# Four attention layers on one core: the output projection read from dense rows, half the side credit in the last layer, and a rule for unread matmuls

## The chip, the cores and the metric

The kernel runs on one core of a Trainium2 chip. The metric is the device time of one execution in microseconds (us). Three runs of the kernel before took 2326.96, 2328.76 and 2332.97 us; the median is 2328.76 us.

## The reference

The input is x, 2048 tokens of 640 features in bf16. Four layers are added to it in turn, and each is layer norm, attention with 32 heads of 20 features, an output projection, and the residual sum:

```python
def _B_ref(x, wqkv, wo):
    qkv = (x @ wqkv).reshape(B, S, 3, H, Dh) ...          # H = 32, Dh = 20
    scores = jnp.einsum("bhqd,bhkd->bhqk", q, k) * (Dh ** -0.5)
    p = _softmax(scores, axis=-1)
    o = jnp.einsum("bhqk,bhkd->bhqd", p, v)
    return o.transpose(0, 2, 1, 3).reshape(B, S, D) @ wo

x = x + _A_ref(_layernorm(x, axis=-1), A_wqkv, A_wo)      # a mask: 0 <= q - k < 256
x = x + _B_ref(_layernorm(x, axis=-1), B_wqkv, B_wo)      # all keys
x = x + _A_ref(_layernorm(x, axis=-1), A_wqkv, A_wo)
x = x + _B_ref(_layernorm(x, axis=-1), B_wqkv, B_wo)
```

The first and third layers (numbered 0 and 2 below, weights A) see a sliding window of 256 keys; the second and fourth (1 and 3, weights B) see all 2048 keys.

## The kernel before

**Tiling.** The tokens are cut into four chunks of 512 queries (c = 0 to 3), the heads into eight groups of four (g = 0 to 7). A unit is one (layer, chunk, group). Inside a group each head has a strip of 32 partitions: rows 0 to 19 of the strip hold its features, the other twelve are zeros. For one head and 128 keys, a score matmul (line 1253) writes a bank of PSUM of 128 keys x 512 queries. A "tile" is three such banks (two in part of layers 0 and 1, sometimes four in layer 3). One activation on ScalarE (line 1284) takes the exponential of a whole tile, and a second matmul with the values (line 1317) adds it up in bank 7. The value matrix carries a column of ones, so the sum of the exponentials comes with it. Banks 0 to 2 and 3 to 5 take turns as the tile's banks: TensorE fills one set while ScalarE reads the other. Bank 6 alone is left for everything else from the middle of layer 1 on.

**The end of a unit.** `finish_unit` copies bank 7 to `oT` (line 839), and a "tail" (`t_tail`, line 1006) divides by the sums in three steps with small matmuls, ending in a multiplication on VectorE that writes group g of the tile `on` (line 1052).

**The output projection.** `t_out` (line 529) multiplies the eight groups of `on` with the output weights `wop`. Both keep the strips of 32 with their zeros, so the contraction over 640 features is done as eight matmuls of 128 rows of which 80 are in use. A chunk is four blocks of 128 tokens by two halves of 320 columns, 64 matmuls of 128x320 in eight groups of eight (line 541). Every group takes bank 6, and VectorE adds it to x (line 550). For the very last chunk `t_before_last` (line 564) does groups 0 to 5 ahead of the end, and `t_out` the two that remain.

**What sets the order.** Everything is emitted by one loop over tiles. In each turn it emits the tile's score matmuls and its exponential; then `pump` lets the side tasks (projections, layer norm, output projection) run for as long as a credit lasts, which grows by `rate(t)` in each tile; then `keep_clock` runs; then come the value matmuls of earlier tiles. A side task that is inside an accumulation is "held" and is continued whatever the credit, so that the eight matmuls of a group of `t_out` stand in one tile. A task may ask to sleep for some ticks; a tick is one tile.

**Unread matmuls.** `keep_clock` (line 632) counts the TensorE work of the side tasks in a number `heat`. Where `heat` and what was carried over stay under `least` (1.76 for a tile of three banks from layer 1's second half on, 0 from the second chunk of layer 3 on), it adds matmuls of 128x512 whose result nobody reads (`unread`, line 620), as long as bank 6 is free.

**Loads.** The SP queue issues, in the program's order, the loads of queries, keys and values of coming units (lines 745 to 767), the output weights (line 132) and the result (line 556). The POOL queue issues the weights of the projections and the stores of q, k and v.

Of the kernel before, what the change touches and what calls it, by code (L numbers as in the profile page):

```python
# [12 lines left out]
ALU = mybir.AluOpType  # L13
ACT = mybir.ActivationFunctionType

P = 128
# [3 lines left out]
DH = 20  # L20
NT = S // P
KD = D // P
G = 8
C = 512
NC = S // C
EPS = 1e-5
SCALE = DH ** -0.5
HD = D // 2
# [21 lines left out]
def kernel(  # L50
# [75 lines left out]
        nc.sync.dma_start(out=x_sb[:, 4 * c : 4 * c + 4, :], in_=xin[:, 4 * c : 4 * c + 4, :])  # L126
    nc.sync.dma_start(out=wv_sb[1][:], in_=wq_view[1][:, :, 2 * D : 3 * D])

    def load_wop(w):
        v = wo_in[w].rearrange("(g j e) f -> j e g f", g=G, j=4)  # L130
        for j in range(4):
            nc.sync.dma_start(out=wop[32 * j : 32 * j + DH, :, :], in_=v[j])
# [41 lines left out]
    ready = set()  # L174
    todo = []
    tails = []
    state = {"tick": 0, "held": None, "credit": 0.0, "early": True, "act": True, "unit": 0, "heat": 0.0, "carry": 0.0, "least": 0.0}

    class Task:

# [348 lines left out]
    def t_out(l, c):  # L529
        on = ons[l, c]  # L530
        last = (l, c) == (3, NC - 1)
        while last and "before_last" not in ready:
            yield ("wait", 1)
        assert out_seq[out_n[0]] == l % 2
        for qb in range(4):
            for i in range(2):
                mb = yield from take_m()
                yp = ps[:, mb, 0:HD]
                g0 = G - 2 if last else 0
                for g in range(g0, G):  # L540
                    nc.tensor.matmul(  # L541
                        yp, lhsT=on[:, g, qb * P : (qb + 1) * P],
                        rhs=wop[:, g, i * HD : (i + 1) * HD],
                        start=(g == g0), stop=(g == G - 1),
                    )
                    if g < G - 1:
# [3 lines left out]
                nc.vector.tensor_tensor(out=xv, in0=had, in1=yp, op=ALU.add)  # L550
                drop_m(mb)
                yield ("pe", 0.14)
            if l < 3:
                stats(l + 1, c, qb)
            else:
                nc.sync.dma_start(out=xout[:, 4 * c + qb, :], in_=x_sb[:, 4 * c + qb, :])
        ons.pop((l, c))
        ready.add(("out", l, c))
        ready.add(("x", l + 1, c))
        n = out_n[0] = out_n[0] + 1  # L560
        if n < len(out_seq) and out_seq[n] != out_seq[n - 1]:
            load_wop(out_seq[n])

    def t_before_last():

        on = ons[3, NC - 1]
        for qb in range(4):
            for i in range(2):
                mb = yield from take_m()
                yp = ps[:, mb, 0:HD]  # L570
                for g in range(G - 2):
                    nc.tensor.matmul(
                        yp, lhsT=on[:, g, qb * P : (qb + 1) * P],
                        rhs=wop[:, g, i * HD : (i + 1) * HD],
                        start=(g == 0), stop=(g == G - 3),
                    )
                    if g < G - 3:
# [35 lines left out]

    def cool():

        return state["heat"] + state["carry"] < state["least"]

    def unread(b):

        nc.tensor.matmul(  # L620
            ps[:, b, :], lhsT=ident[:], rhs=masks[:, 0, :], start=True, stop=True
        )
        state["heat"] += 1.0
# [8 lines left out]
    def keep_clock():  # L632

        while cool():
            t = choose(False)
            if t is not None and state["credit"] > -0.5:
                state["credit"] -= advance(t)
                continue
            b = min(mfree, key=mfree.get)
            if mfree[b][0] > state["tick"]:  # L640
                break
            unread(b)
        spare = state["heat"] + state["carry"] - state["least"]
        state["carry"] = min(max(spare, 0.0), 3.0)
        state["heat"] = 0.0
# [360 lines left out]
    def t_tail(l, c, g, on, oT):  # L1006
# [40 lines left out]
        for qb in range(4):  # L1047
# [16 lines left out]
    def t_zeros():  # L1064

        z = ka_all[:, G : G + 4, :].rearrange("p a b -> p (a b)")
        yield ("wait", 4)
        for n in range(2):
            nc.gpsimd.dma_start(
                out=wop[:, 4 * n : 4 * n + 3, :].rearrange("p g f -> p (g f)"), in_=z[:, 0 : 3 * D]  # L1070
            )
            nc.gpsimd.dma_start(out=wop[:, 4 * n + 3, :], in_=z[:, 0:D])
            yield ("wait", 1)
        load_wop(0)
# [71 lines left out]
    with tc.manual_schedule():  # L1146
# [49 lines left out]
        def rate(t):  # L1196

            if t >= len(tiles):
                return 0.9
            u = tiles[t][0][0]  # L1200
            if index[u.l, u.c, u.g, u.part] < woven:
                return 1.2
            done, r = 0.0, 0.6 if state["early"] else 0.3
            for task in todo:
                done += max(task.left, 0.0)
                if task.need < len(units):
                    r = max(r, done / max(starts[id(units[task.need])] - t - 16, 1))
            return min(1.1 * r, 1.0 if u.l == 0 else 0.9)
# [10 lines left out]
        while ended is None or t < ended + 8:  # L1219
# [3 lines left out]
            if t < len(tiles) or banks:  # L1223
# [23 lines left out]
                if n_b == 4:  # L1247
                    mseq[0] += 1
                    mfree[6] = (state["tick"] + 2, mseq[0])
                for n in range(2):  # L1250
                    for i, (u, j, m, b0, subs, first, last, end) in enumerate(cur):
                        for kc, q0, qn, col in subs[n : n + 1]:
                            nc.tensor.matmul(  # L1253
                                sp[:, i, col * P : (col + qn) * P],
                                lhsT=u.k(kc, j), rhs=u.q(j, q0, qn), start=True, stop=True,
                            )
# [137 lines left out]
```

## Time and profile before

| | |
|---|---|
| profiled execution | 2335.83 us |
| its span, first to last instruction | 2334.1 us |
| ScalarE (ACT) busy | 2177.3 us, 93% |
| TensorE (PE) busy | 2019.9 us, 87% |
| VectorE (DVE) busy | 1465.6 us, 63% |
| mean granted TensorE clock | 0.852 |
| output projection, line 541 | 976 matmuls of 128x320 |
| unread matmuls, line 620 | 788 of 128x512 |

A busy time is the union of an engine's recorded instructions. The profile records an instruction with its whole latency, so that neighbours overlap; how fast an engine goes is read from the distance between starts. "PEclk" is the share of full speed that TensorE's clock was granted. A line of the waits names who waited, for whom, the sum in us, how often, and the longest.

### The profile page before, as it was taken

The numbers are of one execution on the slowest core, as the hardware profiler recorded it, in microseconds if no ns is written. First come the engines' busy times: TensorE is split into PE (matmuls) and PEld (weight loads), VectorE is DVE, ScalarE is ACT, GpSimd is POOL, SyncE is SP. The second block draws the span as 40 slices with busy tenths as digits, with TensorE's granted clock in tenths as the row PEclk, the third lists the DMA queues.
The fourth block names the chain that finished last, engine by engine and source line by source line (L and its number), as shares of the span: only waits on it lengthen the run. The fifth ranks groups of instructions, "written<-read, shape, count | busy, mean of one in ns | idle before, by whom it ended". The sixth has DMA issues, their size and how long they took to land.

```text
span 2334.1 us, 40627 instructions
## 1 busy us (share of the span) xinstructions
PE 2019.9 (87%) x15793; PEld 725.3 (31%) x15793; DVE 1465.6 (63%) x2726; ACT 2177.3 (93%) x1751; POOL 273.7 (12%) x445
## 2 busy tenths in 40 slices
PE   8899999988899888888988898898878888888887
PEld 3344333333323332233322333342322122222222
DVE  6677776426646666666666544452677777777772
ACT  6788889999999998999899899999999999999997
POOL 4332321201100012000120013001000000000000
PEclk9999999999989999999999999999855565556556
DMA  6232322322200123102230023112200010011100
GB/s 189 82 88 79 100 75 64 83 64 65 83 19 27 46 69 95 48 14 55 75 103 25 18 84 107 39 27 78 64 29 27 27 38 27 27 38 37 29 14 12
DMA packets 84881, 132.57 MB, mean 57 GB/s; under 512 B 19760, under 2 KB 60080, under 8 KB 84688
## 3 DMA queue, kind: packets, MB, share of 16 engines
q1 hardware_dynamic: 65472, 76.80, 11.9%
q0 software_dynamic: 19216, 53.17, 7.9%
q8 instruction: 124, 2.03, 0.4%
q14 instruction: 69, 0.57, 0.1%
HBM read 98.70 MB, written 27.79 MB: 54 GB/s over the span
## 4 chain that ended last, share of the span: by engine, by line
ACT 41%; PE 28%; issue 14%; DVE 12%; DMA 1%; POOL 0%; SPq 0%; ACTq 0%; DVEq 0%; POOLq 0%
ACT pt L1284 40%; PE ps L1253 7%; PE ps L354 5%; PE ps L541 4%; PE ps L1317 4%; DVE pt L1353 3%; PE ps L455 3%; PE ps L620 2%; DVE st L304 1%; DVE on L1052 1%; ACT ka L1284 1%; DVE raw_o L887 1%; DVE oT L839 1%; PE ps L419 1%; DVE raw_o L897 1%
## 5 line engine op out<-in xcount | busy, mean ns | idle before, releaser
L1284 ACT ACTIVATE pt<-ps 128x1536 bf16<-128x1536 f32 (+2 forms) x1641 | 2100.2, 1502 | 114.8 <-PE ps L1253 107.0
L1253 PE MATMUL ps<-qt,kt 32*128 32x512 bf16 x4008 | 642.1, 456 | 192.8 <-ACT pt L1284 160.9
L1317 PE MATMUL ps<-pt,vt 128*21 128x512 bf16 x3860 | 466.9, 456 | 0.3 <-ACT pt L1284 0.3
L1253 PEld LDWEIGHTS <-kt 32*128 32x128 bf16 x4008 | 190.4, 94 | 610.8 <-issue 589.7
L1353 DVE TENSOR_TENSOR pt<-pt,masks 128x1024 bf16<-128x1024 bf16 (+5 forms) x403 | 238.0, 624 | 127.3 <-ACT pt L1284 126.8
L620 PE MATMUL ps<-masks,ident 128*128 128x512 bf16 x788 | 270.6, 396 | 28.3 <-DVE rT L1039 11.9
L354 PE MATMUL ps<-xnT,wqk 128*128 128x512 bf16 x830 | 220.2, 390 | 14.2 <-DVE on L1052 3.7
L1317 PEld LDWEIGHTS <-vt 128*21 128x21 bf16 x3960 | 100.0, 90 | 319.8 <-issue 310.6
L304 DVE CAST st<-ps 128x512 bf16<-128x512 f32 x128 | 88.4, 690 | 159.9 <-PE ps L354 159.7
L541 PE MATMUL ps<-wop,on 128*128 128x320 bf16 x976 | 167.6, 315 | 5.5 <-DVE x_sb L550 2.3
L1253 PE MATMUL ps<-qa,ka 32*128 32x384 bf16 (+2 forms) x1408 | 117.6, 277 | 30.6 <-ACT pt L1284 25.8
L887 DVE TENSOR_SCALAR xnT<-ps 128x512 int32<-128x512 f32 x88 | 60.8, 690 | 106.6 <-PE ps L880 106.2
L1052 DVE TENSOR_TENSOR on<-oT,ps 128x512 bf16<-128x512 bf16 x128 | 87.3, 682 | 59.9 <-PE ps L1048 57.3
L839 DVE CAST oT<-ps 128x512 bf16<-128x512 f32 x112 | 76.7, 685 | 73.4 <-PE ps L1317 49.1
L550 DVE TENSOR_TENSOR x_sb<-x_sb,ps 128x320 bf16<-128x320 bf16 x120 | 57.9, 482 | 100.3 <-PE ps L541 100.0
L455 PE MATMUL ps<-wv,xnT 128*128 128x320 bf16 x640 | 108.6, 302 | 10.4 <-DVE rz L1025 3.8
L541 PEld LDWEIGHTS <-on 128*128 128x128 bf16 x976 | 90.5, 101 | 71.6 <-issue 37.3
L354 PEld LDWEIGHTS <-wqk 128*128 128x128 bf16 x830 | 71.0, 98 | 110.4 <-issue 52.2
L620 PEld LDWEIGHTS <-ident 128*128 128x128 bf16 x788 | 59.3, 97 | 130.5 <-issue 128.6
L388 POOL TENSOR_SCALAR rstd<-mv 128x4 f32<-128x4 f32 x15 | 4.9, 328 | 794.1 <-DVE mv L375 794.1
L1317 PE MATMUL ps<-pt,va 128*21 128x384 bf16 (+2 forms) x1408 | 79.5, 283 | 6.9 <-DVE pt L1353 5.5
L1253 PEld LDWEIGHTS <-ka 32*128 32x128 bf16 x1408 | 44.3, 92 | 98.2 <-issue 89.8
(107 smaller groups left out, 1794.4 us busy)
## 6 DMA issues: line engine op xcount, KB each, us to landing
vt<-v_d SPq DMA_DIRECT2D x48, 336.0 KB
kt<-k_d SPq DMA_DIRECT2D x192, 80.0 KB
wqk<-in_B_wqkv_dram POOLq DMA_DIRECT2D x80, 160.0 KB, 3.9
wqk<-in_A_wqkv_dram POOLq DMA_DIRECT2D x70, 160.0 KB, 3.5
k_d<-st POOLq DMA_DIRECT2D x75, 128.0 KB, 2.2
q_d<-st POOLq DMA_DIRECT2D x75, 128.0 KB, 2.2
qt<-q_d SPq DMA_DIRECT2D x384, 20.0 KB
v_d<-vs POOLq DMA_DIRECT2D x16, 336.0 KB, 3.1
```

What stands on the lines that cost most here:

```text
L304: nc.vector.tensor_copy(out=out_, in_=in_)
L354: nc.tensor.matmul(pq, lhsT=wt[:, dc, :], rhs=xt[:, dc, :], start=(dc == 0), stop=(dc == KD - 1),)
L455: nc.tensor.matmul(pv, lhsT=xt[:, dc, i * P : (i + 1) * P], rhs=wv_sb[l % 2][:, dc, h * HD : (h + 1) * HD], start=(dc == 0), stop=(dc == K ...
L541: nc.tensor.matmul(yp, lhsT=on[:, g, qb * P : (qb + 1) * P], rhs=wop[:, g, i * HD : (i + 1) * HD], start=(g == g0), stop=(g == G - 1),)
L620: nc.tensor.matmul(ps[:, b, :], lhsT=ident[:], rhs=masks[:, 0, :], start=True, stop=True)
L839: nc.vector.tensor_copy(out=oT[:], in_=op)
L887: V.tensor_scalar(out=xi.bitcast(I32)[:, i * C : (i + 1) * C], in0=side["psum"], scalar1=SCALE * LOG2E * E23, scalar2=127.0 * E23, op0=ALU ...
L1052: nc.vector.tensor_tensor(out=on[:, g, :], in0=oT[:], in1=zb, op=ALU.mult)
L1253: nc.tensor.matmul(sp[:, i, col * P : (col + qn) * P], lhsT=u.k(kc, j), rhs=u.q(j, q0, qn), start=True, stop=True,)
L1284: nc.scalar.activation(out=pt[:, i:k, b0 * P :], in_=sp[:, i:k, b0 * P :], func=ACT.Exp, scale=SCALE,)
L1317: nc.tensor.matmul(op[32 * j : 32 * j + VW, q0 * P : (q0 + qn) * P], lhsT=u.v(kc, j), rhs=pg[:, i, col * P : (col + qn) * P], start=(first ...
L1353: nc.vector.tensor_tensor(out=pt_[:, i:k, b0 * P :], in0=pt_[:, i:k, b0 * P :], in1=mv_, op=ALU.mult,)
```

## The change

Four things are changed.

1. From layer 1 on, `on` holds the 640 features densely, as five blocks of 128 rows. The multiplication at the end of a tail writes one of three free slots of `on` (5 to 7), and two ticks later SP issues four or five transfers within SBUF that move each head's 20 rows to their dense place (a head that crosses a block's edge takes two). After the last group of a chunk three more ticks pass before the chunk counts as done. `t_out` then needs five matmuls in a group where it had eight, and `t_before_last` four where it had six. The last two groups of the last chunk keep the old form. `load_wop` loads the weights densely from then on.
2. In the last layer the side tasks' credit grows by 0.45 in a tile where it grew by 0.9.
3. `cool` has a second rule: from the second chunk of layer 1 on, until `least` is 0, a tile whose own work is under 0.9 gets an unread matmul, whatever was carried over from earlier tiles.
4. Where bank 6 is not free for an unread matmul, it is "owed", and is emitted in front of the next tile's score matmuls, into the first of the banks that they are about to write.

```diff
-    def load_wop(w):
+    def packed(l, c):
+
+        return l > 0
+
+    def load_wop(w, dense):
+        if dense:
+            nc.sync.dma_start(out=wop[:, 0:KD, :], in_=wo_in[w].rearrange("(b p) f -> p b f", p=P))
+            if w and out_n[0] == 4:
+                v = wo_in[w].rearrange("(g j e) f -> j e g f", g=G, j=4)
+                for j in range(4):
+                    nc.sync.dma_start(
+                        out=wop[32 * j : 32 * j + DH, G - 2 : G, :], in_=v[j][:, G - 2 : G, :]
+                    )
+            return
...
+        dense = packed(l, c) and not last
+        a, b = (0, KD) if dense else (G - 2 if last else 0, G)
         for qb in range(4):
             for i in range(2):
...
-                for g in range(g0, G):
+                for g in range(a, b):
...
-        if n < len(out_seq) and out_seq[n] != out_seq[n - 1]:
-            load_wop(out_seq[n])
+        if n < len(out_seq) and (n == 4 or out_seq[n] != out_seq[n - 1]):
+            load_wop(out_seq[n], n >= 4)
...
-                for g in range(G - 2):
+                for b in range(4):
+                    n = min(P, (G - 2) * 80 - b * P)
...
     def cool():
 
+        if state["least"] > 0.0 and state["heat"] < state["floor"]:
+            return True
         return state["heat"] + state["carry"] < state["least"]
...
             b = min(mfree, key=mfree.get)
-            if mfree[b][0] > state["tick"]:
+            if state["early"] and mfree[b][0] > state["tick"]:
                 break
-            unread(b)
+            if mfree[b][0] > state["tick"] - (0 if state["early"] else 0):
+                state["owed"] += 1
+                state["heat"] += 1.0
+            else:
+                unread(b)
...
-        nc.vector.tensor_tensor(out=on[:, g, :], in0=oT[:], in1=zb, op=ALU.mult)
+        end = (l, c) == (3, NC - 1) and g >= G - 2
+        spread = packed(l, c) and not end
+        nu = on[:, 5 + g % 3 if spread else g, :]
+        nc.vector.tensor_tensor(out=nu, in0=oT[:], in1=zb, op=ALU.mult)
         drop_m(mb)
         yield ("pe", 0.3)
         fill(3)
+        if spread:
+            yield ("wait", 2)
+            for j in range(4):
+                r, a = (4 * g + j) * DH, 0
+                while a < DH:
+                    b, o = divmod(r + a, P)
+                    n = min(DH - a, P - o)
+                    nc.sync.dma_start(
+                        out=on[o : o + n, b, :], in_=nu[32 * j + a : 32 * j + a + n, :]
+                    )
+                    a += n
+            if g == G - 1 or (l, c, g) == (3, NC - 1, G - 3):
+                yield ("wait", 3)
...
             if t >= len(tiles):
-                return 0.9
+                return 0.45
...
+                while state["owed"]:
+                    state["owed"] -= 1
+                    nc.tensor.matmul(
+                        sp[:, 0, :], lhsT=ident[:], rhs=masks[:, 0, :], start=True, stop=True
+                    )
...
+                state["floor"] = 0.9 if state["unit"] >= index[1, 1, 0, None] else 0.0
```

More of the change, by code (lines that the diff above doesn't have):

```diff
@@ L176 @@
     tails = []
-    state = {"tick": 0, "held": None, "credit": 0.0, "early": True, "act": True, "unit": 0, "heat": 0.0, "carry": 0.0, "least": 0.0}
+    state = {"tick": 0, "held": None, "credit": 0.0, "early": True, "act": True, "unit": 0, "heat": 0.0, "carry": 0.0, "least": 0.0, "floor": 0.0, "owed": 0}
     class Task:
@@ L538, in t_out @@
                 yp = ps[:, mb, 0:HD]
-                g0 = G - 2 if last else 0
-                for g in range(g0, G):
+                for g in range(a, b):
                     nc.tensor.matmul(
@@ L543, in t_out @@
                         rhs=wop[:, g, i * HD : (i + 1) * HD],
-                        start=(g == g0), stop=(g == G - 1),
+                        start=(g == a), stop=(g == b - 1),
                     )
-                    if g < G - 1:
+                    if g < b - 1:
                         yield ("hold", 0.14)
@@ L570, in t_before_last @@
                 yp = ps[:, mb, 0:HD]
-                for g in range(G - 2):
+                for b in range(4):
+                    n = min(P, (G - 2) * 80 - b * P)
                     nc.tensor.matmul(
-                        yp, lhsT=on[:, g, qb * P : (qb + 1) * P],
-                        rhs=wop[:, g, i * HD : (i + 1) * HD],
-                        start=(g == 0), stop=(g == G - 3),
+                        yp, lhsT=on[0:n, b, qb * P : (qb + 1) * P],
+                        rhs=wop[0:n, b, i * HD : (i + 1) * HD],
+                        start=(b == 0), stop=(b == 3),
                     )
-                    if g < G - 3:
+                    if b < 3:
                         yield ("hold", 0.14)
@@ L1073, in t_zeros @@
             yield ("wait", 1)
-        load_wop(0)
+        load_wop(0, False)
         for t in (*kts, *qts):
```

## The prediction

> **What bounds the kernel now.** I read the page first: the busy shares, the chain that ended last and the groups.
>
> ```profile
> PE 2019.9 (87%) x15793; PEld 725.3 (31%) x15793; DVE 1465.6 (63%) x2726; ACT 2177.3 (93%) x1751; POOL 273.7 (12%) x445
> PEclk9999999999989999999999999999855565556556
> ACT 41%; PE 28%; issue 14%; DVE 12%; DMA 1%; POOL 0%; SPq 0%; ACTq 0%; DVEq 0%; POOLq 0%
> L1284 ACT ACTIVATE pt<-ps 128x1536 bf16<-128x1536 f32 (+2 forms) x1641 | 2100.2, 1502 | 114.8 <-PE ps L1253 107.0
> L541 PE MATMUL ps<-wop,on 128*128 128x320 bf16 x976 | 167.6, 315 | 5.5 <-DVE x_sb L550 2.3
> ```
>
> ScalarE's exponentials are the bound, and the only thing that holds them up is TensorE being late with scores: 107.0 us over the span. No change to TensorE's work can give more than what ScalarE loses there. The clock row says that TensorE runs at half clock in most of the last 30%, yet ScalarE is full in those slices. So I asked where the loss lies, by stretches (columns: PE, PEld, DVE, ACT, POOL busy, clock, DMA share, GB/s).
>
> ```profile
> 583.50:700.20 116.70, 102.99 (x771) 33.54 (x768) 62.60 (x117) 109.27 (x94) 11.30 (x16) 0.93 0.18 51
> 700.20:816.90 116.70, 102.01 (x855) 38.85 (x855) 76.13 (x151) 115.95 (x101) 3.31 (x6) 1.00 0.14 37
> 1700.00:1888.00 188.00, 154.74 (x956) 38.25 (x956) 142.04 (x205) 188.00 (x138) 0.00 (x0) 0.50 0.10 29
> 1888.00:1912.00 24.00, 21.56 (x157) 9.39 (x156) 17.51 (x26) 18.92 (x15) 0.00 (x0) 0.84 0.13 43
> ```
>
> In the last layer ScalarE is 188.00 of 188 busy at half clock with no side work, and 18.92 of 24 where a chunk's output projection runs. In layers 1 and 2 two stretches of equal length lose 7.4 us at clock 0.93 and 0.75 us at 1.00. The timeline of ScalarE prices the first kind:
>
> ```profile
> 1885.58 5.71 ACT L1284 ACTIVATE pt<-ps 128x1536 bf16<-128x1536 f32 x4
> 1892.91 1.45 ACT L1284 ACTIVATE pt<-ps 128x1536 bf16<-128x1536 f32 x1 [1.62 <-PE ps L1253]
> 1894.76 1.45 ACT L1284 ACTIVATE pt<-ps 128x1536 bf16<-128x1536 f32 x1 [0.39 <-PE ps L1253]
> 1896.60 8.34 ACT L1284 ACTIVATE pt<-ps 128x1536 bf16<-128x1536 f32 x6 [0.39 <-PE ps L1253]
> 1906.17 1.45 ACT L1284 ACTIVATE pt<-ps 128x1536 bf16<-128x1536 f32 x1 [1.23 <-PE ps L1253]
> 1908.22 2.97 ACT L1284 ACTIVATE pt<-ps 128x1536 bf16<-128x1536 f32 x2 [0.61 <-PE ps L1253]
> 1911.89 2.79 ACT L1284 ACTIVATE pt<-ps 128x1536 bf16<-128x1536 f32 x2 [0.70 <-PE ps L1253]
> ```
>
> Elsewhere eleven exponentials in a row take 14.69 us (from 1099.13), so one starts every 1.335 us. From 1885.58 to 1911.89 there are 15 starts: 26.3 - 15 x 1.335 = 6.3 us lost.
>
> [...] stretches read 1.00 or 0.50, and eight matmuls of L541 start to end in 2.29 us at 1889.71 and in 1.26 us at 1892.74. [...] a dense block should cost what a padded one costs, for which no run yet has both. [...] the stores of q and k (128 KB) land 2.2 us after issue here.
>
> **The change part by part.** The instruction lists of the two built programs give counts. L541 goes from 976 to 712 matmuls, L572 from 48 to 32, unread ones from 788 to 854, and 102 more stand in score banks; SP gets 423 transfers more. Scores, values, exponentials and evictions keep their numbers, but for one tile more in the last layer.
>
> Dense rows and half pace, last layer. Lost as above: 6.3 us for chunk 1; 20 starts from 1662.79 to 1695.25, 5.8 for chunk 0; 19 from 2101.27 to 2132.59, 6.0 for chunk 2; 7 from 2269.80 to 2283.00, 3.9 for the early part of chunk 3: 22.0 in all. With eight matmuls in a tile the exponentials start 1.84 us apart at full clock (1892.91, 1894.76, 1896.60), and 2.4 to 2.5 at half (2113.32 to 2115.68 and 2130.08 to 2132.59 in chunk 2). Five take 0.79 us instead of 1.26 at full clock: 1.84 - 0.47 = 1.37, almost nothing lost. At half they take 1.43 instead of 2.29: 2.5 - 0.86 = 1.64, so 0.3 lost. In the new order a group stands in about two tiles of three, with gaps, so the clock wakes later: I take five groups of eight cold, 1.5 us, and 0.7 for the tiles at the turns, 2.2 us for each chunk, and 1.2 for chunk 3 (four matmuls a group, 1.14 us cold). That leaves 8 of 22: **-14 us**, between -9 (all cold, and each late by twice as much) and -20 (none lost).
>
> Dense rows, layers 1 and 2. Eight chunks lose 24 matmuls each, 3.8 us of TensorE at 0.158. Groups of eight mostly stand in every second tile at full clock and cost ScalarE nothing (1099.13: eleven exponentials without a gap beside four such groups). Only where they meet a cold clock do they count: **-2 us**, 0 to -6.
>
> The floor and the owed matmuls. The waits view gives 52.4 us of ScalarE's waits between 350 and 1667. Of the 19 slices of the page from 525 to 1634, asked for as stretches, nine are under full clock; ScalarE idles 40 us in them, and 8 us in the ten at full clock. Some of the 40 is side work that would be late anyway. In the order after, owed matmuls stand in the tiles just ahead of two of these places (670 to 680 and 1304 to 1312, where tails with one unread matmul a tile follow each other and the clock falls). Others (at 571 and at 1121, where TensorE waits for VectorE's layer norm rows) the floor doesn't touch. I take a quarter of the 33 us between the two kinds: **-9 us**, between +6 and -22. The bound above zero: 168 matmuls more, at 0.158 x 512/320 = 0.25 us, are 42 us of TensorE. In poor tiles they are covered: TensorE's side work is some 0.4 us of a tile there. Where that cover is gone, one seventh on ScalarE's path is +6. One in a score bank delays that tile's scores by 0.25 us; scores have a whole tile, 1.335 us, before they are late.
>
> The packing. SP issues a transfer each 0.37 us (1632.32, 1632.71, 1633.11 ...), so a group adds 1.5 to 1.9 us to its queue. Behind them stand the loads of coming units, which are issued a unit ahead. At most 20 SP transfers stand in six tiles, 7.4 us of 8.0 (17 before), so the queue keeps up. The first transfer waits for VectorE's multiplication, the fourth-next multiplication for the slot; both are long done. For the last group: the small matmuls ran at 1887.97, the multiplication ended at 1889.66, 1.7 us; five issues 1.9; landing 2.2, an estimate from the stores: 5.8 us. The projection comes five ticks after the small matmuls, 6.7 us: 0.9 to spare. If SP has a unit's nine loads ahead (3.4 us), TensorE stalls 2.5 us with scores queued behind, and ScalarE, one tile behind, 1.2 us. Twelve occasions: **+2 us**, 0 to +15. The chain to the next layer starts three or four ticks later (first L541 of layer 1's second chunk at tile 525, 521 before), which its slack of many tiles covers.
>
> Sum: -14 - 2 - 9 + 2 = -23 us on the profiled 2335.8 (span 2334.1 and 1.7 around it): 2313. The profiled execution is 7 us over the median of the runs, 2328.76, so a run should show **2306 us**.
>
> **The rivals.**
> A, as above: 2306, its own range 2298 to 2314; chance 0.42.
> B, the clock falls in layers 1 and 2 as before: the floor's heat is counted, not busy time, and TensorE waiting for VectorE stays idle. Then -14 - 2 + 3 = -13: 2316 (2310 to 2321); for it speaks that tiles with two unread matmuls went cold too (679); chance 0.24.
> C, the clock stays awake everywhere: -20 - 6 - 22 + 2 = -46 at most, taken at -35: 2294; the stalls on VectorE speak against; chance 0.10.
> D, the extra unread matmuls fall where TensorE is behind and cost +6, packing +6, and the last layer gives only -9: about 2330, no change; chance 0.12.
> E, slower: packed rows land late. Every chunk's first group then stands on TensorE in front of the scores. Break-even with A's 25 us of gains: 2.1 us of ScalarE at each of twelve occasions, so a landing 0.9 + 1.3 + 2.1 = 4.3 us later than taken, some 6.5 us after issue. A transfer of 20 rows has no such time in this trace, but 20 KB loads between DRAM and SBUF have no landing shown at all; 2345; chance 0.12.
>
> **How the numbers follow.** A measurement tells 0.3%, 7 us, from no change. A, B and C are faster (0.76), D same (0.12), E slower (0.12). From 2294 to 2332 holds A, B, half of C and most of D.
>
> **What would show it.** Right: lost time in the last layer's four bursts near 8 us instead of 22; L555 at 712; ScalarE's waits between 350 and 1667 near 42 us, and fewer slices there under full clock; no wait of TensorE on a transfer into `on`. Wrong: a PE wait named after the packing DMA, or half-clock stretches in layers 1 and 2 that start in poor tiles as before.

## The result

The kernel after takes 2328.62 us (median of 4 runs, 2326.06 to 2330.96), the kernel before 2330.69 us in runs beside it (2326.96 to 2332.97). The ratio is 0.9992, 95% interval [0.9974, 1.0011]: no difference that can be measured, where 2306 was forecast. The profiled execution took 2328.77 us, with a span of 2327.1.

The page of the kernel after, the lines that answer to those of before:

```profile
PE 2000.7 (86%) x15515; PEld 705.3 (30%) x15681; DVE 1464.4 (63%) x2726; ACT 2177.9 (94%) x1752; POOL 276.0 (12%) x445
PEclk9899999998999999999999989999765555556556
L1326 ACT ACTIVATE pt<-ps 128x1536 bf16<-128x1536 f32 (+2 forms) x1644 | 2103.7, 1479 | 109.4 <-PE ps L1295 103.7
L555 PE MATMUL ps<-wop,on 128*128 128x320 bf16 x712 | 129.3, 315 | 7.3 <-DVE x_sb L564 4.3
```

The projection's matmuls are the 712 of the forecast, yet the exponentials wait for scores 103.7 us where it was 107.0. (TensorE's busy time is not set against that of before: this profile has 15515 matmuls for 15681 weight loads, so 166 have no record.) ScalarE's waits, first between 350 and 1667 us, then from 1667 to the end:

```profile
ACT pt L1326 <- PE ps L1295: 58.2, 100, 3.0
...
ACT pt L1326 <- PE ps L1295: 8.7, 16, 1.2
```

Before, the same two answers were 52.4 and 17.4. The gain in the last layer is there; in layers 1 and 2, where some 10 us were to go, 6 us were added. (Three more profiles with the code of before in this stretch, from the runs below, give 46.9 to 50.6.) The two stretches of equal length that the prediction set side by side, now (same columns):

```profile
583.50:700.20 116.70, 100.04 (x791) 34.90 (x804) 64.41 (x119) 113.38 (x99) 10.93 (x16) 1.00 0.21 57
700.20:816.90 116.70, 103.12 (x843) 37.63 (x851) 76.90 (x154) 115.43 (x99) 3.67 (x7) 1.00 0.15 42
```

In the first the clock went from 0.93 to 1.00 and ScalarE from 109.27 to 113.38: here the change did what it says. But the waits rose elsewhere. Since every exponential can be counted off against its tile, all profiles can be cut at the same tiles: 350 (layer 1, chunk 1) and 1150 (layer 3, chunk 0), in us. A tile counts as "at half clock" below when the mean granted clock from its exponential's start to the next tile's is under 0.75.

| kernel | to tile 350 | 350 to 1150 | from 1150 | tiles at half clock, 350 to 1150 |
|---|---|---|---|---|
| before | 530.1 | 1107.1 | 696.9 | 30 |
| after | 529.6 | 1111.9 | 685.5 | 24 |

So -11.4 in the end and +4.8 in the middle. One profile of the middle is not sure to some 9 us (see the first experiment), so the shares were measured by runs.

### The profile page after: what moved, and what is told of

It reads as the page before. It is cut to its first block, busy times and chain, and to the rows that moved or that the text cites. A ratio compares the mean times of both kernels' runs of the same rounds, so it can differ in the third digit from the quotient of the medians.

```text
span 2327.1 us, 40931 instructions
## 1 busy us (share of the span) xinstructions
PE 2000.7 (86%) x15515; PEld 705.3 (30%) x15681; DVE 1464.4 (63%) x2726; ACT 2177.9 (94%) x1752; POOL 276.0 (12%) x445
## 4 chain that ended last, share of the span: by engine, by line
ACT 28%; PE 12%; issue 9%; DVE 4%; DMA 0%; POOL 0%; ACTq 0%; DVEq 0%; POOLq 0%; SPq 0%
ACT pt L1326 27%; PE ps L1295 3%; PE ps L1360 2%; PE ps L555 2%; PE ps L367 1%; PE ps L468 1%; ACT ka L1326 1%; DVE pt L1396 1%; PE ps L637 1%; DVE st L317 1%; DVE x_sb L564 0%; PE ps L901 0%; DVE oT L860 0%; PE ps L432 0%; DVE raw_o L908 0%
## 5 line engine op out<-in xcount | busy, mean ns | idle before, releaser
L1326 ACT ACTIVATE pt<-ps 128x1536 bf16<-128x1536 f32 (+2 forms) x1644 | 2103.7, 1479 | 109.4 <-PE ps L1295 103.7
L1295 PEld LDWEIGHTS <-kt 32*128 32x128 bf16 x4008 | 184.5, 94 | 594.5 <-issue 574.0
L367 PE MATMUL ps<-xnT,wqk 128*128 128x512 bf16 x762 | 210.3, 388 | 17.8 <-DVE st L317 3.5
L555 PE MATMUL ps<-wop,on 128*128 128x320 bf16 x712 | 129.3, 315 | 7.3 <-DVE x_sb L564 4.3
L637 PEld LDWEIGHTS <-ident 128*128 128x128 bf16 x854 | 66.8, 97 | 145.2 <-issue 142.7
L555 PEld LDWEIGHTS <-on 128*128 128x128 bf16 x712 | 62.9, 101 | 62.5 <-issue 41.1
L531 POOL DMA_DIRECT2D k_d<-st x75 | 42.2, 563 | 269.2 <-DVE st L317 221.2
```

The lines of the kernel that those rows point to most:

```text
L367: nc.tensor.matmul(pq, lhsT=wt[:, dc, :], rhs=xt[:, dc, :], start=(dc == 0), stop=(dc == KD - 1),)
L555: nc.tensor.matmul(yp, lhsT=on[:, g, qb * P : (qb + 1) * P], rhs=wop[:, g, i * HD : (i + 1) * HD], start=(g == a), stop=(g == b - 1),)
L637: nc.tensor.matmul(ps[:, b, :], lhsT=ident[:], rhs=masks[:, 0, :], start=True, stop=True)
L1295: nc.tensor.matmul(sp[:, i, col * P : (col + qn) * P], lhsT=u.k(kc, j), rhs=u.q(j, q0, qn), start=True, stop=True,)
L1326: nc.scalar.activation(out=pt[:, i:k, b0 * P :], in_=sp[:, i:k, b0 * P :], func=ACT.Exp, scale=SCALE,)
```

## The experiments

The theory after the result: the last layer gives about what was forecast, and both the dense rows in layers 1 and 2 and the new rule for unread matmuls ("the floor" from here on) cost time. Rivals: that the last layer gave nothing and the profile is chance; that one of the two parts in the middle gains and the other costs more. All were timed beside the kernel before (medians of before 2328.4 to 2329.9). In the code cuts, "..." marks lines left out.

**Half pace alone**, the kernel before with:

```diff
-                return 0.9
+                return 0.45
```

> The kernel before with the last layer's credit at 0.45 alone. Groups of eight stay whole, 1.12 of credit each, so one stands in every two to three tiles. If pace is what spared the last layer, its four bursts lose 12 us instead of 22 and the time is about 2321 (before: 2330.7). If dense rows are, the groups of eight now all start on a half clock at 1.0 to 1.3 us each, 8 x 1.2 x 3 = 29 us, and the time is about 2340.

Ratio 0.9989 [0.998, 0.9998], -2.5 us: neither the 2321 nor the 2340. (The 0.45 acts from the second chunk of layer 3 on, which is where all projections of that layer stand.) From tile 1150 it takes 694.8 us, 2.1 less than before. Up to there it is the same program as before, and yet the middle took 1098.4 us in its profile against 1107.1: identical code differs by 8.7 us from one execution to another.

Where it differs can be seen. Four of the profiles have the code of before up to tile 1150 (before, this one, and two of a kernel below). Of the 32 blocks of 25 tiles between 350 and 1150, 20 are at full clock in all four (under 1 us at half clock), and 19 of these take the same time to 0.1 us; the twentieth, 0.6 apart, comes right behind a block where the clock fell in all four. The rest of the difference stands in the 12 blocks where it fell in at least one. The 25 tiles from 450, first of before, then of this run (columns as in the prediction):

```profile
667.27:703.83 36.56, 33.34 (x222) 9.18 (x222) 16.99 (x34) 32.79 (x28) 0.00 (x0) 0.81 0.04 10
665.71:698.35 32.64, 27.45 (x219) 9.34 (x221) 16.88 (x34) 31.83 (x27) 0.00 (x0) 1.00 0.04 11
```

The single executions, each with its mean clock, say the same. Of 75 of the kernel before, timed beside this run and the next three, the 12 at a mean clock of 0.852 or less took 2335.4 us on average, the 9 at 0.857 or more 2325.0. Counting half-clock time as 2 x (1 - mean clock) x span, a straight line through the 75 gives 0.32 us for each us at half clock (correlation 0.90). This is used below, as an estimate of 0.3: it says what goes together in one program, and no run sets the clock alone.

**Dense rows alone**, the kernel after without floor and owed matmuls, with the old pace:

```diff
-            if mfree[b][0] > state["tick"] - (0 if state["early"] else 0):
-                state["owed"] += 1
...
+            unread(b)
...
-                return 0.45
+                return 0.9
...
-                state["floor"] = 0.9 if state["unit"] >= index[1, 1, 0, None] else 0.0
+                state["floor"] = 0.0 if state["unit"] >= index[1, 1, 0, None] else 0.0
```

> Dense rows with their grace alone, credit 0.9, no floor and no owed matmuls. Theory P (the packed output projection of layers 1 and 2 comes later and in smaller groups, and costs there what it saves in the last layer): -8 in the last layer, +8 in layers 1 and 2, about 2331. Theory F (the floor's and the owed matmuls are what costs): -8 and -2, about 2321.

Ratio 0.9978 [0.9966, 0.9989], between the two theories. From tile 1150: 687.7 us, 9.2 under before. The program has 849 unread matmuls, 61 more than before, all between tiles 350 and 1150: five matmuls add less to `heat` than eight, and the old rule makes up for some of that.

**Floor and owed matmuls alone**, the kernel before with parts 3 and 4 of the change:

```diff
+        if state["least"] > 0.0 and state["heat"] < state["floor"]:
+            return True
...
+                state["owed"] += 1
...
+                state["floor"] = 0.9 if state["unit"] >= index[1, 1, 0, None] else 0.0
```

> The floor and the owed matmuls alone. Theory P: the stretches of half clock in poor tiles go, nothing else changes, -9, about 2322. Theory F: 168 more unread matmuls cost more than the clock gives, +7, about 2338.

Ratio 1.0029 [1.0019, 1.0039]: +6.8 us where the prediction had -9. Its middle has 11 tiles at half clock against 30. The clock got what it was to get, and yet the time rose. Its 22 runs have a mean clock of 0.860 against 0.854, 24 us less at half clock, which is worth some 7 us by the estimate of 0.3. So its 141 unread matmuls more (929 with the owed ones, 788 before) and the order that goes with them cost about 14 us. In its profile the 19 blocks at full clock take 4.0 us more than in the four with the code of before, and the other 13, with 30 us less at half clock, the same time. ScalarE's waits between 350 and 1667 don't show it, with 48.1 us: the exponentials overlap in the records (1.45 us long, 1.33 apart), so a start that is a tenth of a us late leaves no idle time.

**Dense rows with half pace**, the kernel after with

```diff
-                state["floor"] = 0.9 if state["unit"] >= index[1, 1, 0, None] else 0.0
+                state["floor"] = 0.0 if state["unit"] >= index[1, 1, 0, None] else 0.0
```

and without the owed matmuls:

> The change without the floor and the owed matmuls. Theory P: -11 in the last layer and +8 in layers 1 and 2, about 2328, within 0.3% of the kernel before. Theory F: -11 and -2, about 2318.

Ratio 0.9976 [0.9964, 0.9987], -5.6 us; from tile 1150 686.4 us. Half pace adds nothing measurable to dense rows. With the floor's +6.8 this sums to +1.2 us, inside the interval of the kernel after (-6 to +3).

**Dense rows and grace (the three ticks at the end of a chunk) in layer 3 only, half pace**, without floor and owed matmuls:

```diff
     def packed(l, c):
 
-        return l > 0
+        return l > 2
```

(and the dense load of the weights eight chunks later)

> Dense rows and their grace in layer 3 alone, credit 0.45 there, no floor; layers 1 and 2 as in the kernel before. If packing costs some 4.5 us in layers 1 and 2 and gives 10.5 in layer 3, the time is 10.5 us under the kernel before, about 2318, ratio 0.9955. If the gap between the last layer's gain and the total was chance, it is as e4_dense_pace, ratio 0.9976.

Ratio 0.9953 [0.9933, 0.9973], and 0.9954 [0.994, 0.9968] when repeated:

> The same kernel as the one with dense rows and their grace in layer 3 alone and half pace there, measured before at 0.9953 [0.9933, 0.9973]. If the gain of the last layer is what carries it, the chip makes no difference: 0.994 to 0.997. If the earlier run was lucky in the clock phases of layers 1 and 2: 0.998 to 1.000.

2318.9 us both times: this beats both kernels. Its gain over before, -10.7 us, is the last layer's. Against the run with dense rows in all three layers (-5.6), the dense rows and the packing in layers 1 and 2 cost some 5 us (1 to 9 with both intervals), where -2 and a part of +2 were forecast. Part of it goes with the clock: that run has 8 to 13 us more at half clock (mean clock 0.852, here 0.854 and 0.853), 2 to 4 us by the estimate of 0.3. In its profile the 19 blocks at full clock are 3.2 us shorter than with the code of before, and the other 13 are 7.9 us longer, with 14 us more at half clock.

**Two places where it costs.** The first: the timeline of the kernel with dense rows in three layers and half pace, at a layer norm ahead of layer 2's projections; in brackets the idle time ahead and what ended it:

```profile
833.82 0.87 POOL L331 DMA_DIRECT2D wqk<-in_A_wqkv_dram  x1 [2.98 <-PE ps L367]
834.77 0.19 POOL L401 TENSOR_SCALAR rstd<-mv 128x4 f32<-128x4 f32 x1
835.04 1.03 POOL L404 TENSOR_TENSOR rstd<-rstd,nhalf 128x4 f32<-128x4 f32 x1
836.11 0.16 DVE L407 SCALAR_TENSOR_TENSOR nmr<-mv,rstd 128x4 f32<-128x4 f32 x1 [2.86 <-POOL rstd L404]
837.43 0.27 PE L1054 MATMUL ps<-ident,hl 128*32 128x128 bf16 x1 [3.58 <-DVE st L317]
838.77 1.45 ACT L1322 ACTIVATE pt<-ps 128x1536 bf16<-128x1536 f32 x1 [3.36 <-PE ps L1291]
```

GpSimd's queue holds a weight load that waits 2.98 us, until TensorE has read the buffer's old weights. Behind it stand the two instructions of layer norm's reciprocal square root; VectorE waits 2.86 us for them, TensorE 3.58 for VectorE, and ScalarE 3.36 for scores. In the kernel before, GpSimd issued its loads of these weights 43 us ahead of this layer norm (796.00 and 838.87), and nothing stood in front of it. Tile 580 takes 4.82 us in both profiles with dense rows in layer 1 and no floor, and 1.33 in the one of before. To try the reason, the loads were issued after the reciprocal, in the kernel with dense rows and half pace:

```diff
-        for n in (1, 0):
-            order = worder[l, n]
-            if order and not any(e in wtiles for e in order):
-                wtiles[order[0]] = get_w(*order[0])
...
         nc.gpsimd.tensor_tensor(out=rstd[:], in0=rstd[:], in1=nhalf[:], op=ALU.pow)
+        for n in (1, 0):
+            order = worder[l, n]
+            if order and not any(e in wtiles for e in order):
+                wtiles[order[0]] = get_w(*order[0])
         yield ("wait", 2)
```

> e4_dense_pace with one edit: GpSimd issues the first weight loads of a layer norm's chunk after the two small instructions of that layer norm and not ahead of them. In e4_dense_pace a weight load waits 2.98 us for TensorE in front of the layer norm on GpSimd, VectorE waits 2.86 us for it, TensorE 3.58 us for VectorE, ScalarE 3.36 us. If that chain is most of packing's cost in layers 1 and 2, 3 to 4 us come back: ratio 0.9960. If not, 0.9976 stays.

Ratio 0.9964 [0.9954, 0.9975] against 0.9976: some 3 of the 5 us, but the intervals leave room for chance. The place itself is shown: tile 580 takes 1.39 us, and the 25 tiles from 575 take 37.5 us where they took 42.5 (36.3 before). Nor was the layer norm late: freed of the load, its reciprocal runs in tile 577 (834.59), in the kernel before in tile 580. But the next 50 tiles take 74.8 us where they took 70.2, so that from 525 to 650 nothing is gained in these profiles (178.8 and 178.4; before 177.1). What the rest of the 5 us is made of stays open.

The second place is the start of layer 3, in the run without this edit (dense rows in three layers, half pace):

```profile
1365.16 0.39 PE L1291 MATMUL ps<-qt,kt 32*128 32x512 bf16 x1 [2.54 <-DMA kt<-k_d]
1365.65 1.45 ACT L1322 ACTIVATE pt<-ps 128x1536 bf16<-128x1536 f32 x1 [2.11 <-PE ps L1291]
```

The scores of tile 956 wait 2.54 us for layer 3's keys. The chain that leads to them does come later here: the output projection stands in tiles 928 to 936 (before 924 to 933), the reciprocal behind it in tile 937 (934), the two stores of keys ahead of this wait in tiles 955 and 956 (953 and 954). All four profiles with dense rows in layers 1 and 2 and the grace have this wait, of 2.3 to 2.9 us; their tiles 956 and 957 take 6.7 to 7.5 us together, against 3.4 to 3.5 in the four with the code of before. (Some of it is made up for nearby: the 50 tiles from 925 take 77.3 to 80.1 us against 73.0 to 76.8.) The edit above leaves this place as it was, with a wait of 2.84 us.

With the packing in layer 3 alone, the same edit is no good:

> Dense rows in layer 3 alone with half pace (earlier run 0.9953), and GpSimd's weight loads issued after the layer norm's reciprocal square root. If the loads ahead of the reciprocal cost time only where the chain to the next layer starts late: no change, 0.995. If they cost some in every layer: 0.994 or less, below 2317 us.

Ratio 0.9983 [0.9965, 1.0002], against 0.9953 without it. The loads are now late for others: TensorE waits 4.0 us for weights (1.1 in the repeated run without it). That is 3 us of some 7; the rest is open.

**Without the grace** in layers 1 and 2:

```diff
-            if g == G - 1 or (l, c, g) == (3, NC - 1, G - 3):
+            if l == 3 and (g == G - 1 or (c, g) == (NC - 1, G - 3)):
```

> The kernel with dense rows and half pace (no floor, nothing owed; earlier run 0.9976), with the three ticks' grace only in layer 3. If the grace is what makes the next layer's start late and costs some 4 to 5 us in layers 1 and 2: about 0.996, 2320 us, and layers 1 and 2 within 2 us of before. If the transfers or the order of the loads cost it: no change from 0.9976, and layers 1 and 2 stay 4 us longer than with dense rows in layer 3 alone. If rows land late without the grace: TensorE waits for a transfer into on, and it is slower than 0.9976.

Ratio 1.0088 [1.0064, 1.0111], 26 us more than with the grace. It can't be done without: TensorE waits 13.0 us in six places for the packed rows, and the mean clock falls from 0.852 to 0.844, 43 us more at half clock, which the estimate of 0.3 puts at 13 us. Its tiles 956 and 957 take only 2.7 us, with no wait for keys, which fits the grace as what makes that chain late; its order differs in more than this, though. One of the six waits, in the timeline of this kernel:

```profile
753.90 0.69 DVE L1072 TENSOR_TENSOR on<-oT,ps 128x512 bf16<-128x512 bf16 x1 [0.43 <-PE ps L1065]
...
755.84 0.76 PE L555 MATMUL ps<-wop,on 128*128 128x320 bf16 x4
759.17 0.31 PE L555 MATMUL ps<-wop,on 128*128 128x320 bf16 x1 [2.57 <-DMA on<-on]
...
760.45 1.45 ACT L1322 ACTIVATE pt<-ps 128x1536 bf16<-128x1536 f32 x1 [2.30 <-PE ps L1291]
```

The multiplication ends at 754.59, the rows are there at 759.17: 4.6 us for the issues and the landing, where the prediction had worked out 4.1.

**What of the floor costs.** The kernel before with the floor, without the owed matmuls:

```diff
+        if state["least"] > 0.0 and state["heat"] < state["floor"]:
+            return True
...
+                state["floor"] = 0.9 if state["unit"] >= index[1, 1, 0, None] else 0.0
```

> The kernel before with the floor, and nothing owed: where bank 6 is taken, the tile stays without. If the matmuls in score banks are what costs (they stand in front of the scores), the time is that of the kernel before or less, ratio 0.998 to 1.000. If the cost is that the floor lets side work run ahead of its credit and adds matmuls in tiles of two banks, it stays near e3_floor, 1.003.

Ratio 1.0023 [1.0007, 1.0038], not told apart from the 1.0029 with them: the owed ones alone are not the cost. Without pulling side work ahead on the floor's account, so that it puts in unread matmuls instead (floor and owed matmuls as in the change):

```diff
-            if t is not None and state["credit"] > -0.5:
+            due = state["heat"] + state["carry"] < state["least"]
+            if due and t is not None and state["credit"] > -0.5:
```

> The kernel before with the floor and the owed matmuls, but a side task is run ahead of its credit only where the old rule asks for work; the floor alone adds unread matmuls. If the pulled side work is what costs, ratio 0.998 to 1.000. If the matmuls are, near e3_floor, 1.003.

Ratio 1.0047 [1.0029, 1.0065]: worse, with 11 tiles at half clock again. Next the floor's own 191 unread matmuls at a quarter of their columns, nothing owed:

```diff
+        k = 512 if state["heat"] + state["carry"] < state["least"] else 128
         nc.tensor.matmul(
-            ps[:, b, :], lhsT=ident[:], rhs=masks[:, 0, :], start=True, stop=True
+            ps[:, b, 0:k], lhsT=ident[:], rhs=masks[:, 0, 0:k], start=True, stop=True
         )
```

> The kernel before with the floor and nothing owed, as the earlier run at 1.0023, and the same order of all instructions; but the 191 unread matmuls that only the floor asks for are 128x128 in place of 128x512. Nothing that the reference asks for is left out. Theory 1 (the array time of the unread matmuls, put into tiles with no room for them, is what the floor costs): three quarters of it is gone, so the ratio falls from 1.0023 to about 1.0005, 2330 us. Theory 2 (the order that the floor makes, side work pulled ahead and unread matmuls that wait for VectorE to empty bank 6, is what it costs): size does not matter, 1.002 to 1.003, about 2335 us. Theory 3 (the full clock that these matmuls bring is a gain inside a larger loss): with a quarter of the work the clock falls more, the ratio is above 1.0023.

Ratio 1.0117 [1.0094, 1.0141], and 75 tiles at half clock: what theory 3 said. It does not decide between 1 and 2, since most of the 191 stand in place of others that the old rule would have put in (848 unread in all, 788 before), so that it took heat away. The 102 us more at half clock (mean clock 0.834 and 0.854) are some 31 us by the estimate of 0.3, and it lost 27. And without any unread matmul from layer 1's second chunk on, 218 in place of 788:

```diff
-                state["least"] = warmth * n_b / 3 if state["unit"] < index[3, 1, 0, None] else 0.0
+                state["least"] = warmth * n_b / 3 if state["unit"] < index[1, 1, 0, None] else 0.0
```

> The kernel before without any unread matmul from layer 1's second chunk on: 218 are left of 788. Nothing that the reference asks for is left out. Theory of the prediction (TensorE at half clock makes ScalarE late, so that keeping the clock awake is worth time): ScalarE's waits between the tiles 350 and 1150 rise by 15 us or more, about 2345 us. Rival (where no side work stands, half clock costs ScalarE nothing, and where it stands the unread matmuls take room): within 5 us of before or faster, 2320 to 2330 us.

Ratio 1.0208 [1.0187, 1.0229], +48 us, with a mean clock of 0.741 where before has 0.854. Keeping the clock awake is worth much. But not everywhere: two stretches of 25 tiles each of this kernel (tiles 475 and 725 on),

```profile
702.33:733.55 31.22, 26.92 (x190) 7.42 (x189) 19.47 (x40) 31.05 (x30) 0.00 (x0) 0.50 0.09 25
1056.32:1095.98 39.66, 33.53 (x220) 12.12 (x216) 20.17 (x38) 33.27 (x25) 0.00 (x0) 0.72 0.07 20
```

and the same tiles of the kernel before:

```profile
703.83:734.90 31.07, 27.95 (x230) 9.49 (x230) 19.59 (x40) 30.92 (x30) 0.00 (x0) 1.00 0.09 26
1043.23:1075.70 32.47, 26.87 (x224) 11.02 (x220) 20.68 (x40) 32.47 (x27) 0.00 (x0) 1.00 0.10 30
```

The first runs wholly at half clock and takes 31.22 us, against 31.07 at full; so do the 25 tiles from 1050, with 33.46 against 33.54. The second, in which side work begins again on a clock that has fallen, takes 7.2 us more. Here a stretch at half clock costs 0.15 us or less where ScalarE stays full (31.05 of 31.22 us busy), and 0.32 of itself in the line through the 75 runs.

**Adding alone.** In none of these is the floor's work apart from the order it makes. So: the kernel before in its own order, with unread matmuls only added, in tiles whose own heat is under 0.9 and where bank 6 is free, not counted in the old rule:

```diff
         spare = state["heat"] + state["carry"] - state["least"]
+        heat = state["heat"]
+        b = min(mfree, key=mfree.get)
+        while 0.0 < state["least"] and heat < state["floor"] and mfree[b][0] <= state["tick"]:
+            nc.tensor.matmul(
+                ps[:, b, 0:512], lhsT=ident[:], rhs=masks[:, 0, 0:512], start=True, stop=True
+            )
+            heat += 1.0
...
+                state["floor"] = 0.9 if state["unit"] >= index[1, 1, 0, None] else 0.0
```

> The kernel before with the order of all its instructions untouched; in tiles of layers 1 to 3 whose own TensorE work is under 0.9 an unread 128x512 matmul is added where bank 6 is free, 85 in all, which count for nothing in the rule for the others. Theory 1 (array time): 85 x 0.25 us = 21 us of TensorE, of which a fifth to a third shows, 1.002 to 1.003, some 2334 us. Theory 2 (the floor's new order of side work and of the other unread matmuls costs, the matmuls themselves are good for the clock): no loss, 0.997 to 1.000, fewer cold tiles between 340 and 1150 than the kernel before. Theory 3 (waits for bank 6): 1.002 to 1.003, with waits of the added line for VectorE of 5 us or more.

Then of 128 columns (`0:128` for `0:512`), and with a floor of 1.9 in place of 0.9:

> As the run with 85 unread matmuls added in the order of the kernel before, but of 128x128. Theory 1: a quarter of its loss, 1.0005 to 1.001. Theory 2: as before, 0.999 to 1.000, because a quarter of the work warms little. Theory 3: the same loss as with 128x512, 1.002 to 1.003.

> As the run with 85 unread matmuls added in the order of the kernel before, with the floor at 1.9 in place of 0.9: 213 are added. Theory 1: two and a half times the loss, 1.005 to 1.008, some 2345 us. Theory 2: the clock full in nearly all tiles between 340 and 1150, no loss or a gain, 0.995 to 1.000. Theory 3: 1.005 or more, with waits of the added line for VectorE of 10 us or more.

| kernel | added | ratio | us over before | us for each added |
|---|---|---|---|---|
| 128x512 | 85 | 1.0032 [1.002, 1.0045] | 7.5 | 0.09 |
| 128x128 | 85 | 1.0013 [1.0003, 1.0023] | 3.0 | 0.04 |
| 128x512, floor 1.9 | 213 | 1.0066 [1.0052, 1.008] | 15.4 | 0.07 |

This is theory 1 in the main: the cost goes with number and size, about a third of the 0.25 us that one takes on TensorE (1.24 us for five matmuls of this size, in the timeline below). Theory 3's sign, waits for VectorE of 5 us or more, is there too (see below), and the interval of the small ones just reaches its 1.002. Five blocks of 25 tiles (from 350, 550, 600, 800 and 975) have no tile at half clock in any of the four profiles; together they take 180.1 us before, and 185.1, 182.4 and 189.0 in the three. With 24, 24 and 49 added matmuls in them, one of 512 columns costs some 0.2 us there.

The floor itself fits the same price, whether it changes the order or not. The clock's share is taken out with the estimate of 0.3:

| kernel | unread 128x512 more than before | us over before | us at half clock, against before | estimate for one matmul, us |
|---|---|---|---|---|
| floor, nothing owed | 60 | 5.4 | -9 | 0.14 |
| floor and owed | 141 | 6.8 | -24 | 0.10 |
| floor and owed, no side work pulled | 189 | 10.9 | -28 | 0.10 |
| added | 85 | 7.5 | -6 | 0.11 |
| added, floor 1.9 | 213 | 15.4 | -5 | 0.08 |

How it comes about, first TensorE of the kernel before near tile 982:

```profile
1403.71 1.24 PE L354 MATMUL ps<-xnT,wqk 128*128 128x512 bf16 x5
1404.88 0.39 PE L1253 MATMUL ps<-qt,kt 32*128 32x512 bf16 x3
1405.20 0.40 PE L1317 MATMUL ps<-pt,vt 128*21 128x512 bf16 x4
1405.53 0.39 PE L1253 MATMUL ps<-qt,kt 32*128 32x512 bf16 x3
```

and of the kernel with 85 added:

```profile
1404.49 1.24 PE L354 MATMUL ps<-xnT,wqk 128*128 128x512 bf16 x5
1405.66 0.39 PE L1260 MATMUL ps<-qt,kt 32*128 32x512 bf16 x3
1406.51 0.38 PE L647 MATMUL ps<-masks,ident 128*128 128x512 bf16 x1 [0.46 <-DVE st L304]
1406.82 0.40 PE L1325 MATMUL ps<-pt,vt 128*21 128x512 bf16 x4
1407.15 0.39 PE L1260 MATMUL ps<-qt,kt 32*128 32x512 bf16 x3
```

The five matmuls of a projection (1.24 us) make their tile too long, and the tile behind it, poor in work, is where TensorE catches up: 0.65 us from one tile's scores to the next. With the added matmul it is 1.49 us, of which 0.46 is a wait for VectorE to empty bank 6, and the next exponential starts 0.13 us later after its predecessor than it did. The added matmuls' own groups in the profiles of the two sizes show that this wait does not go by size, the rest does:

```profile
L647 PE MATMUL ps<-masks,ident 128*128 128x512 bf16 x85 | 32.4, 381 | 11.4 <-DVE st L304 4.5 <-DVE x_sb L550 3.1 <-DVE vs L304 0.4
```

```profile
L647 PE MATMUL ps<-masks,ident 128*128 128x128 bf16 x85 | 18.8, 221 | 11.3 <-DVE st L304 4.4 <-DVE x_sb L550 3.1 <-DVE vs L304 0.4
```

The kernel after has the same sign: its unread matmuls (854 in the program, 757 of them recorded) wait for VectorE's `st`, 6.8 us in 18 places, and those of the kernel before do not.

## Why the prediction was wrong

**Last layer, -14 forecast: right, a size off.** The timeline of ScalarE in the kernel after, chunk 1's projection:

```profile
1868.82 35.12 ACT L1326 ACTIVATE pt<-ps 128x1536 bf16<-128x1536 f32 x26
1904.56 1.45 ACT L1326 ACTIVATE pt<-ps 128x1536 bf16<-128x1536 f32 x1 [0.61 <-PE ps L1295]
1906.68 14.88 ACT L1326 ACTIVATE pt<-ps 128x1536 bf16<-128x1536 f32 x11 [0.68 <-PE ps L1295]
1922.25 1.45 ACT L1326 ACTIVATE pt<-ps 128x1536 bf16<-128x1536 f32 x1 [0.69 <-PE ps L1295]
1923.85 6.92 ACT L1326 ACTIVATE pt<-ps 128x1536 bf16<-128x1536 f32 x5
```

From the last start of the first row, 1902.49, to 1923.85 there are 14 starts: 21.4 - 14 x 1.335 = 2.7 us lost, where it was 6.3 and 2.2 were forecast. By the same count the four bursts lose 2.8, 2.7, 3.4 and 0.9: 9.8 us against 22.0 before and 8 forecast. So 12 saved, and 11.4 in the section. (The distance of 1.335 us counts the last exponential with its whole latency; from start to start it is 1.32, which adds 0.1 to 0.3 us to each burst before and after.) What the prediction had not seen is that the dense rows do it: the pace adds nothing to them that could be measured. A dense block costs what a padded one does, as it assumed: weight loads of 98 ns and matmuls of 299 ns in the median, for the 976 padded ones of before and for the 440 dense ones among the 712 of after.

**Dense rows in layers 1 and 2 with their packing, -2 and +2 forecast, some +5 measured: wrong.** The step that failed is the last of the packing: beyond rows that land late, the new order is put at nothing, as something "which its slack of many tiles covers". At full clock the dense rows gave about what was forecast (3.2 us in the 19 blocks). But the 13 other blocks, in which no wait for rows stands either, are 7.9 us longer, with 14 us more at half clock. At the start of layer 3 the slack was not there: the chain comes two to four tiles later, the keys are late by 2.3 to 2.9 us, and two tiles take over 3 us more, in all four such profiles. At tile 580 it is not slack that failed, since the layer norm there is not late: a weight load stands in front of it on GpSimd and holds ScalarE up for 3.36 us. How the 5 us divide among these two places, the 61 more unread matmuls and the colder clock stays open.

**Lateness of packed rows: right in kind.** No wait of TensorE for packed rows appears after; without the grace there are six, of 2.2 us on average, and the 4.1 us worked out were 4.6. Rival E's case, rows that land late, is the run without the grace.

**The floor and the owed matmuls, -9 forecast: wrong in sign, +6.8 measured.** The step that failed is "in poor tiles they are covered: TensorE's side work is some 0.4 us of a tile there". A mean over poor tiles hides that some stand right behind a rich one, whose surplus TensorE works off in them (at tile 982, behind a projection's 1.24 us, 0.65 us from one tile's scores to the next). An unread matmul was not free but cost about 0.1 us, some 14 us for the 141 of the floor; the upper end, "one seventh on ScalarE's path is +6", had the mechanism, but by this estimate two fifths are on the path. The other half of the term held: tiles at half clock went from 30 to 11, worth some 7 us by the estimate, near the 9 forecast (a quarter of 33 is 8). And of the 168 matmuls counted for the floor, 61 come with the dense rows.

So the low clock does cost time (some 7 us for 24 us at half clock), but its cure cost twice as much (some 14). Taking 570 unread matmuls away lost 48 us, adding 85 lost 7.5; nothing in between was tried.

**The sum.** -10.7 (last layer) + 5 (dense rows and packing in layers 1 and 2) + 6.8 (floor and owed) = +1 us, measured -2 with an interval of -6 to +3. Rival D, with extra unread matmuls at +6, packing at +6 and the last layer at -9, was the case that came; it had 0.12. What the prediction held against it was only that a poor tile has room. Of its signs, ScalarE's waits between 350 and 1667 were to fall to 42 us and rose to 58.2. That speaks of the dense rows, whose two runs without the floor have 60.0 and 56.3, and not of the floor, with 48.1. 712 matmuls, and no wait for rows, held.

## What to carry to other kernels

Work that fills an engine was not free here where that engine had not caught up (some 0.1 us for each unread matmul, 0.13 us behind the projection at tile 982): look at the order of starts in the tile concerned and in the one before it, not at the mean load of its kind. Ask of a low clock whether anything waits in that stretch (31.22 us at half clock against 31.07 in one, 39.66 against 32.47 in another), and price the cure as well as the illness, before paying to raise it. When the order of steps changes, list what each is now queued behind on each engine, GpSimd's DMA issues among them (one held ScalarE up for 3.36 us here); and try a change of several parts also without the part that touches most tiles.

## What the hardware showed that was not expected

Identical code in the middle 800 tiles took 1107.1, 1098.4, 1100.4 and 1103.8 us in four profiles, with 61, 41, 48 and 55 us at half clock, and 19 of the 20 blocks at full clock agreed to 0.1 us. Why the clock turned at other places in the same program was not shown. So a single profile of this kernel does not settle 5 us over such a section; the runs' intervals do, and a comparison of the blocks that are at full clock in both.
